# Block products (seven in place of eight) for the second FFN product in three of twelve chunks, and another order of splitting the attention probabilities

## Chip, core and metric

One core of a Trainium2 chip runs the whole program. The metric is the device time in microseconds (us), the median of three runs. Engines: PE is TensorE, DVE VectorE, ACT ScalarE, POOL GpSimd, SP the queue that issues DMAs.

## What is computed

The inputs are q, k, v of shape 4 x 8 x 768 x 64 (q and k are drawn eight times larger than usual) and the two FFN weights, 512 x 2048 and 2048 x 512. Everything is float32.

```
k_sum = k.reshape(B, H, 24, 32, D).max(axis=3);  v_sum = v.reshape(B, H, 24, 32, D).mean(axis=3)
scores = concat([where(|i - j| < 16, scale * q k^T, -1e9), scale * q k_sum^T + log(32)])
x = softmax(scores) @ concat([v, v_sum])          # heads side by side: 3072 tokens x 512
h = x @ w_in
out = (h * sigmoid(h)) @ w_out
```

## The kernel before

**Tiling.** The 3072 tokens are 12 chunks of 256 (CH). The hidden dimension is 16 tiles of 128 (NFT), called f here. For each chunk c and each f, `job_f` (L799) makes the first product (`ffn1`, L812): h, 128 hidden by 256 tokens, in one PSUM bank. Chunk 0 uses float32 matmuls. Every later chunk splits both operands in two float16 parts, high and low, and takes three of the four products, so a first product is 12 matmuls of 256 columns (L818). Then ACT writes t = tanh(h) (L842), DVE makes t = (t + 1) * h (L843), ACT rounds t to its high part gh (L845) and DVE subtracts to get the low part gl (L846). The second product (`ffn2`, L820) takes the two halves u of 128 tokens as stationary operand and the weight rows of f as the moving one: 3 matmuls of 512 columns for each u (L826). They are summed over the 16 f in two banks (4 and 5). At f = 15 the banks are scaled into a staging tile (L871, L872) and stored (L873).

**PSUM.** There are eight banks of 128 x 512 float32. From chunk 1 on h takes banks 0, 1 and 2 in turn (tag "late h"). Banks 6 and 3 hold scores and 7 the attention output. Bank keys of the plan are (bank, half).

**Attention** for chunk c + 2 runs beside chunk c, so none is left beside chunks 10 and 11. For a tile of 128 tokens the scores are made on PE (L591), masked with their row minimum on DVE (L627), and exponentiated with row sums on ACT (L630). In `job_a` (L609), late part, each of two heads' probabilities is scaled by its reciprocal sum into float16 (`scaled`, on DVE, ACT or POOL: L645, L641, L643) and its low part follows on DVE, head by head (`low`, L674). A DMA transposes both parts (L677). PE multiplies them with v (L709), and the result is split into xh and xl (L725, L726), the moving operand of the first product.

**Weights.** They are loaded and unpacked during chunk 0 (`job_load`, `job_w`), scaled by powers of two (`w_scale`, L775) and split into float16 high and low parts over their own storage (`job_pair`). The float32 copy of each weight tile, wr4[:, f, kind, :512], isn't read after that.

**Order of the work.** Nothing is issued in the order of the code. Each job gives `Plan.op` its possible engines with a cost in ns, what it reads and writes, and a due time made from i = 16 c + f and the offsets in TUNE (L960). `Plan.schedule` (L178) lays all operations out in time by these costs, forward and backward in six rounds; each takes the engine on which it would finish well. `Plan.issue` (L210) then emits them sorted by planned start. Each engine executes its own stream in that order, and waits on semaphores where data or storage needs it. A first product may run ahead of the second product by three f (APART, key "turn"). Costs on DVE and POOL exclude each other in the plan unless an operation says otherwise (port=()).

Of the kernel before, what the change touches and what calls it, by code (L numbers as in the profile page):

```python
# [22 lines left out]
P = 128  # L23
# [7 lines left out]
NKEY = HALF + BLK + NB  # L31
# [15 lines left out]
SHRINK = 2.0 ** -25  # L47
# [177 lines left out]
def local_attn_ffn(ctx: ExitStack, tc: tile.TileContext, qkT, qP, qF, kF, v, vR, vP, w, out):  # L225
    nc = tc.nc
    eng = {"dve": nc.vector, "act": nc.scalar, "pool": nc.gpsimd, "dma": nc.sync}
# [19 lines left out]
    wr4 = wr.rearrange("p (f k c) -> p f k c", f=NFT, k=2)  # L247
# [31 lines left out]
    first = const.tile([P, max(NP * 2 * UW + 8 * DM, 8 * KP)], F16, name="first")  # L279
    half = 8 * P + 8 * KT  # L280
# [328 lines left out]
    def job_a(m, prio):  # L609
# [11 lines left out]
        def sum_key(j, i):  # L621
            return ("sum", i4, j, i)
# [42 lines left out]
        for j, n in enumerate(ns):  # L665
            pk, et = (m + j) % NP, e_t[n]
            pt, (tt, ttk) = p_t[pk], tt_of(m + j)
            pkeys = [("p", pk, i) for i in range(2)]
            for i in range(2):
                plan.op({"dve": 235, "act": 296, "pool": 320}, lambda e, i=i, j=j, pt=pt: scaled(e, pt[:, i, :NKEY], j, i), r=[sum_key(j, i), ("e", n, i)], w=[pkeys[i]], prio=prio)  # L670

            def low(e, pt=pt, et=et, j=j):
                for i in range(2):
                    nc.vector.scalar_tensor_tensor(out=pt[:, i, P:P + NKEY], in0=et[:, i, :], scalar=su4[:, 2 * j + i:2 * j + i + 1], in1=pt[:, i, :NKEY], op0=ALU.mult, op1=ALU.subtract)  # L674

            plan.op({"dve": 510}, low, r=[sum_key(j, i) for i in range(2)] + [("e", n, i) for i in range(2)], w=pkeys, prio=prio)
# [98 lines left out]
    def w_scale(prio):  # L775
        plan.op({"dve": 80}, lambda e: nc.vector.tensor_reduce(out=wx_t, in_=wm_t, axis=AX.X, op=ALU.max), r=[("wm", f, kind) for f in range(NFT) for kind in range(2)], w=["wx"], prio=prio)
        k = sbank()

        def tr(e, k=k):
            for j in range(2):  # L780
                nc.tensor.transpose(out=bank[k][:1, j * P:(j + 1) * P], in_=wx_t[:, j:j + 1], identity=ident)

        plan.op({"pe": 220}, tr, r=["wx"], w=bk(k), prio=prio, cols=256)
        steps = (
            lambda e, k=k: nc.vector.tensor_reduce(out=wc[:, 0:2], in_=bank[k][:1, :2 * P].rearrange("o (a p) -> o a p", a=2), axis=AX.X, op=ALU.max),
            lambda e: nc.vector.tensor_scalar(out=wc[:, 0:2], in0=wc[:, 0:2], scalar1=1e-30, scalar2=None, op0=ALU.max),
            lambda e: nc.vector.tensor_scalar(out=wc[:, 2:4].bitcast(U32), in0=wc[:, 0:2].bitcast(U32), scalar1=0x7F800000, scalar2=None, op0=ALU.bitwise_and),
            lambda e: nc.vector.tensor_scalar(out=wc[:, 6:8], in0=wc[:, 2:4], scalar1=2.0 ** -14, scalar2=None, op0=ALU.mult),
            lambda e: nc.vector.reciprocal(out=wc[:, 4:6], in_=wc[:, 6:8]),
            lambda e: nc.vector.scalar_tensor_tensor(out=wc[:, 7:8], in0=wc[:, 6:7], scalar=1.0 / SHRINK, in1=wc[:, 7:8], op0=ALU.mult, op1=ALU.mult))  # L790
# [8 lines left out]
    def job_f(i, c, f):  # L799
# [138 lines left out]
    for i, (c, f) in enumerate(order):  # L938
        plan.slack = SLACK if i >= SETTLED else {}
        d = c + 2 if c + 2 < NCHUNK else None  # L940
        if d and c and f == 0:
            job_stage(2 * d)
            job_attn(2 * d, True)
            job_stage(2 * d + 1)
        plan.slack = {"pe": GATE_SLACK} if i >= SETTLED else {}
        job_f(i, c, f)
        plan.slack = SLACK if i >= SETTLED else {}
        if c == 0 and f == NFT - 1:
            spare[0] = 1
# [72 lines left out]
```

## Time and profile before

| | us |
|---|---|
| median of 3 runs (599.81 to 600.15) | 599.84 |
| the profiled execution, its own time | 599.46 |
| its span, first to last instruction | 597.8 |
| PE busy / DVE / ACT / POOL | 588.6 / 440.1 / 372.2 / 108.6 |
| PE idle in the span | 9.2 |

The profile shows one execution. Busy times are sums for an engine; a wait is put down to the event that came last. Rows of a timeline have start, duration, engine, line, operation, operands with shapes, and in brackets the idle time of the engine before it with what ended that. Matmuls overlap in the pipeline, so the next one starts before the printed duration is over. A group's idle time counts the engine's idle just before its instructions.

### The profile page before, as it was taken

The numbers are of one execution on the slowest core, as the hardware profiler recorded it, in microseconds if no ns is written. First come the engines' busy times: TensorE is split into PE (matmuls) and PEld (weight loads), VectorE is DVE, ScalarE is ACT, GpSimd is POOL, SyncE is SP. The second block draws the span as 40 slices with busy tenths as digits, with TensorE's granted clock in tenths as the row PEclk, the third lists the DMA queues.
The fourth block names the chain that finished last, engine by engine and source line by source line (L and its number), as shares of the span: only waits on it lengthen the run. The fifth ranks groups of instructions, "written<-read, shape, count | busy, mean of one in ns | idle before, by whom it ended". The sixth has DMA issues, their size and how long they took to land.

```text
span 597.8 us, 15304 instructions
## 1 busy us (share of the span) xinstructions
PE 588.6 (98%) x5848; PEld 399.7 (67%) x5848; DVE 440.1 (74%) x1338; ACT 372.2 (62%) x1014; POOL 108.6 (18%) x164
## 2 busy tenths in 40 slices
PE   8999999999999999999999999999999999999997
PEld 5666656676666666666666666666766766666664
DVE  6999979997886748979896555979898764333332
ACT  4998859777757756647675544756777554333332
POOL 3211201035421000043330020014241400000000
PEclk9999999999999999999999999999999999999999
DMA  8999532135765634543646530442734401000001
GB/s 334 410 420 412 174 123 98 27 87 152 153 128 172 157 90 128 90 133 97 123 129 174 166 89 36 120 122 62 169 93 106 111 2 36 36 1 2 35 1 37
DMA packets 60916, 75.29 MB, mean 126 GB/s; under 512 B 41914, under 2 KB 42170, under 8 KB 59050
## 3 DMA queue, kind: packets, MB, share of 16 engines
q1 hardware_dynamic: 60842, 74.31, 41.9%
q8 instruction: 46, 0.75, 0.5%
q14 instruction: 28, 0.23, 0.1%
HBM read 56.79 MB, written 6.29 MB: 106 GB/s over the span
## 4 chain that ended last, share of the span: by engine, by line
PE 82%; DVE 9%; DMA 4%; ACT 3%; issue 1%; SPq 1%; DVEq 0%; ACTq 0%
PE bank L826 37%; PE bank L818 37%; PE bank L709 3%; DVE wm L758 2%; PE bank L591 2%; DVE wr L757 2%; DMA raw<-in_qkT_dram 1%; DMA second<-in_qP_dram 1%; DVE e L627 1%; PE bank L694 1%; ACT wr L771 1%; PE bank L656 1%; DVE t L843 1%; PE bank L837 1%; DMA raw<-in_qF_dram 1%
## 5 line engine op out<-in xcount | busy, mean ns | idle before, releaser
L818 PE MATMUL bank<-x,wr 128*128 128x256 f16 x2112 | 258.1, 273 | 0.0
L818 PEld LDWEIGHTS <-wr 128*128 128x128 f16 x2112 | 205.6, 98 | 57.2 <-issue 0.6
L826 PE MATMUL bank<-wr,gh 128*128 128x512 f16 x702 | 209.1, 380 | 0.4 <-ACT gh L845 0.4
L843 DVE SCALAR_TENSOR_TENSOR t<-t,bank 128x256 f32<-128x256 f32 x192 | 80.1, 417 | 85.9 <-ACT t L842 85.0
L842 ACT ACTIVATE t<-bank,th 128x256 f32<-128x256 f32 x176 | 82.1, 467 | 92.7 <-PE bank L818 92.4
L826 PE MATMUL bank<-wr,gl 128*128 128x512 f16 x351 | 133.1, 379 | 0.1
L845 ACT ACTIVATE gh<-t 128x256 f16<-128x256 f32 x176 | 72.9, 414 | 72.3 <-DVE t L843 69.4
L846 DVE SCALAR_TENSOR_TENSOR gl<-t,gh 128x256 f16<-128x256 f32 x176 | 86.6, 493 | 40.4 <-ACT gh L845 40.0
L826 PEld LDWEIGHTS <-gh 128*128 128x128 f16 x702 | 65.9, 98 | 44.6 <-ACT gh L845 0.7
L630 ACT ACTIVATE e<-e,mx 128x120 f32<-128x120 f32 x192 | 73.2, 383 | 12.9 <-DVE mx L627 12.7
L826 PEld LDWEIGHTS <-gl 128*128 128x128 f16 x351 | 34.3, 98 | 43.7 <-DVE gl L846 3.0
L674 DVE SCALAR_TENSOR_TENSOR first<-e,sum,first 128x120 f16<-128x120 f32 x144 | 49.8, 394 | 0.3 <-POOL first L643 0.3
L643 POOL TENSOR_SCALAR first<-e,sum 128x120 f16<-128x120 f32 x52 | 22.0, 433 | 125.7 <-ACT gh L845 39.6
L627 DVE CUSTOM_DVE_ANT_0 e<-bank,masks,qsc 128x120 f32<-128x120 f32 x144 | 42.2, 336 | 2.8 <-PE bank L591 2.8
L630 ACT ACTIVATION_READ_ACCUMULATOR e<-e,mx 128x1 f32 x192 | 36.4, 190 | 0.0
L238 POOL TENSOR_TENSOR first<-raw,first 120x1024 f16<-120x1024 f32 x14 | 30.4, 2173 | 10.9 <-ACT first L231 5.4
L823 PE MATMUL bank<-wr,t 128*128 128x512 f32 x64 | 30.7, 599 | 0.0
L815 PE MATMUL bank<-x,wr 128*128 128x256 f32 x112 | 26.3, 379 | 0.0
L815 PEld LDWEIGHTS bank<-x,wr 128*128 128x128 f32 x112 | 21.0, 190 | 7.0 <-issue 4.1
L643 POOL TENSOR_SCALAR e<-e,sum 128x120 f32<-128x120 f32 x28 | 11.2, 412 | 71.4 <-DVE sum L636 61.8
L561 POOL TENSOR_SCALAR raw<-raw,vsc 120x1024 f32<-120x1024 f32 x10 | 11.7, 1167 | 55.5 <-PE bank L818 31.0
L773 DVE SCALAR_TENSOR_TENSOR wr<-wr,ws 128x1024 f16<-128x1024 f32 x16 | 20.2, 1274 | 0.1
(146 smaller groups left out, 598.1 us busy)
## 6 DMA issues: line engine op xcount, KB each, us to landing
wr<-in_w_dram SPq DMA_DIRECT2D x14, 1024.0 KB
raw<-in_qkT_dram SPq DMA_DIRECT2D x18, 576.0 KB
out_dram<-raw SPq DMA_DIRECT2D x23, 256.0 KB
raw<-in_kF_dram SPq DMA_DIRECT2D x12, 384.0 KB
raw<-in_qF_dram SPq DMA_DIRECT2D x9, 512.0 KB
raw<-in_vR_dram SPq DMA_DIRECT2D x12, 384.0 KB
raw<-in_v_dram SPq DMA_DIRECT2D x18, 208.0 KB
raw<-in_v_dram SPq DMA_DIRECT2D x18, 192.0 KB
```

The source lines that it names most:

```text
L627: plan.op({"dve": 262 if b else 206}, lambda e, i=i, j=j, et=et, mx=mx: nc.vector.tensor_tensor_reduce(out=et[:, i, :], in0=sc[j][:, i, :N ...
L630: plan.op({"act": 385}, lambda e, i=i, j=j, et=et, mx=mx: nc.scalar.activation(out=et[:, i, :], in_=et[:, i, :], func=AF.Exp, scale=-1.0, ...
L643: nc.gpsimd.tensor_scalar(out=out, in0=src, scalar1=by, scalar2=0.0, op0=ALU.mult, op1=ALU.add)
L674: nc.vector.scalar_tensor_tensor(out=pt[:, i, P:P + NKEY], in0=et[:, i, :], scalar=su4[:, 2 * j + i:2 * j + i + 1], in1=pt[:, i, :NKEY], o ...
L815: nc.tensor.matmul(out=h, lhsT=wi[:, ct * P:(ct + 1) * P], rhs=x0[:, ct, :], start=(ct == 0), stop=(ct == NCT - 1))
L818: nc.tensor.matmul(out=h, lhsT=wip[:, part, ct * P:(ct + 1) * P], rhs=x[:, ct, :], start=(ct == 0 and q == 0), stop=(ct == NCT - 1 and q = ...
L823: nc.tensor.matmul(out=bank[ob[u]], lhsT=t[:, u * P:u * P + P], rhs=wo, start=opens, stop=closes)
L826: nc.tensor.matmul(out=bank[ob[u]], lhsT=g[:, u * P:u * P + P], rhs=wop[:, part, :], start=(opens and q == 0), stop=(closes and q == 2))
L842: plan.op({"act": 264 if c == 0 else 360}, lambda e: nc.scalar.activation(out=t, in_=h, func=AF.Tanh, scale=0.5 if c == 0 else th[:, 0:1]) ...
L843: plan.op({"dve": 337}, lambda e: nc.vector.scalar_tensor_tensor(out=t, in0=t, scalar=1.0, in1=h, op0=ALU.add, op1=ALU.mult), r=bk(k), w=[ ...
L845: plan.op({"act": 311}, lambda e: nc.scalar.activation(out=gh, in_=t, func=AF.Copy, scale=SHRINK), r=[("t", j)], w=[("gh", n)], prio=post)
L846: plan.op({"dve": 343}, lambda e: nc.vector.scalar_tensor_tensor(out=gl, in0=t, scalar=SHRINK, in1=gh, op0=ALU.mult, op1=ALU.subtract), r= ...
```

## The change

**Second product in chunks 8, 9 and 10.** `job_fast` replaces `job_f` there and works on pairs of f. The second product of a pair is a 2 x 2 block product: token halves by the two f on the left, the two f by column halves (256 columns each) on the right. Eight block products are replaced by seven, with sums of blocks on both sides. On the left t of both f is kept in float32 (both f's h lie in the halves of bank 0), three blocks are split directly (hd, ld, 384 columns) and four sums of blocks are formed on POOL or DVE and split (hs, ls, 512 columns). On the right `job_quad` prepares four sums of weight blocks for each pair, between i = 88 and 116 by its place in the loop, and splits them into the storage of the float32 weights. The seven results, each 3 matmuls of 256 columns a pair, are summed over the eight pairs in 3.5 banks (1, 2, 4 and half of 5; in chunk 10: 3, 6, 7 and half of 5). At the end of a chunk one copy and four DVE additions combine them into the four output blocks; two stores follow. A pair's first products may start when the third pair before it is done ("turn").

**Probabilities.** Scaling is done in place in float32, then one operation copies both heads to the high part and one subtraction makes both low parts.

**Others.** The scale of the weights leaves two more bits of room, all values of TUNE differ, and "quad" is new.

```diff
+FAST = 8
+EARLY = 40
+PACE = 4
...
             for i in range(2):
-                plan.op({"dve": 235, "act": 296, "pool": 320}, ... scaled(e, pt[:, i, :NKEY], j, i), r=[sum_key(j, i), ("e", n, i)], w=[pkeys[i]], prio=prio)
-
-            def low(e, pt=pt, et=et, j=j):
-                for i in range(2):
-                    nc.vector.scalar_tensor_tensor(out=pt[:, i, P:P + NKEY], in0=et[:, i, :], scalar=..., in1=pt[:, i, :NKEY], op0=ALU.mult, op1=ALU.subtract)
-
-            plan.op({"dve": 510}, low, ..., w=pkeys, prio=prio)
+                plan.op({"dve": 160, "act": 296, "pool": 320}, ... scaled(e, e_t[n][:, i, :], j, i), r=[sum_key(j, i)], w=[("e", n, i)], prio=prio)
+            hi, lo = pt[:, :, :NKEY], pt[:, :, P:P + NKEY]
+            plan.op({"dve": 193, "act": 282, "pool": 360}, lambda e, hi=hi, et=et: copy(e, hi, et), r=ekeys, w=pkeys, prio=prio)
+            plan.op({"dve": 320, "pool": 600}, lambda e, hi=hi, lo=lo, et=et: less(e, lo, et, hi), r=ekeys, w=pkeys, prio=prio)
...
-scalar1=2.0 ** -14   (w_scale)
+scalar1=2.0 ** -12
...
+    def job_quad(g, i, prio):
+        fa, fb = 2 * g, 2 * g + 1
...
+        for n, x, y in ((0, b12, b11), (2, b22, b12), (1, b22, t[0]), (3, b21, t[1])):
+            plan.op({"pool": 740, "dve": 400}, lambda e, n=n, x=x, y=y: less(e, t[n], x, y), ...)
+        plan.op({"act": 990, "dve": 603}, ... hi = flat * by ...)
+        plan.op({"dve": 1196}, ... lo = flat * by - hi ...)
+
+    acc = {6: (0, 0), 2: (0, 1), 7: (1, 0), 5: (1, 1), 4: (2, 0), 3: (2, 1), 1: (3, 0)}
+    threes = [(1, 2, 4, 5)] * (NCHUNK - 2) + [(3, 6, 7, 5)]
...
+    def job_fast(i, c, f):
+        n, z, b = i % 2, c % 2, c * CH // S
+        g, j, th = f // 2, i // 2 % 3, th_t[b % 2]
+        h, hk = bank[0][:, n * CH:n * CH + CH], [("bank", 0, n)]
...
+        plan.op({"pe": 1312}, ffn1, r=[...] + [("turn", i - 5 - n)], w=hk, prio=i + nudge("f1", i), cols=3072, fill=fill)
+        plan.op({"act": 360}, ... tu = tanh(h) ..., r=hk + [...], w=tk, prio=post)
+        plan.op({"dve": 337}, ... tu = (tu + 1) * h ..., r=hk, w=tk, prio=post, port=())
+        if n == 0:
+            return
...
+        plan.op({"act": 430}, ... hd = src * SHRINK ..., r=tks, w=[("hd", j)], prio=post)
+        plan.op({"dve": 470}, ... ld = src * SHRINK - hd ...)
+        for m, x, y, op in ((0, a21, a22, ALU.add), (2, a11, a21, ALU.subtract), (1, sm[:, 0], a11, ALU.subtract), (3, a12, sm[:, 1], ALU.subtract)):
+            plan.op({"pool": 470, "dve": 210}, ..., r=tks, w=[("sm", j)], prio=post)
+        plan.op({"act": 540}, ... hs = sf * SHRINK ...)
+        plan.op({"dve": 610}, ... ls = sf * SHRINK - hs ...)
...
+                    for q, (x, p) in enumerate(((hi, 0), (hi, 1), (lo, 0))):
+                        nc.tensor.matmul(out=acc_of(c, m)[0], lhsT=x[:, left[m]], rhs=right[m](p), ...)
...
+        for ms, need in (((1,), direct), ((2, 6), ...), ((7, 5), ...), ((4, 3), ...)) if opens or closes else (((1, 4, 2), direct + mixed[2:]), ((6, 7, 5, 3), mixed + direct)):
+            ends = [("turn", i - 1), ("turn", i)] if ms[-1] == 3 else []
+            plan.op({"pe": 328 * len(ms)}, products(ms), ..., prio=late, cols=768 * len(ms))
+        if not closes:
+            return
...
+        plan.op({"act": 300, "dve": 332}, ... s1 = m1 * by ...)
+        plan.op({"dve": 660}, add(rows[:, 1:3], both(ka), spread(s1)), ...)
+        plan.op({"dve": 660}, add(u34, both(kb), spread(rows[:, 1])), ...)
+        plan.op({"dve": 393}, add(rows[:, 1], acc_of(c, 5)[0], u34[:, 0]), ...)
+        plan.op({"dve": 660}, add(rows[:, 0:4:3], both(kd), u34), ...)
...
-        job_f(i, c, f)
+        if i == NFT:
+            release("areas", [("wf", x, 0) for x in range(NFT)], FAST * NFT - TUNE["quad"])
+        g, rest = divmod(i - FAST * NFT + EARLY, PACE)
+        if 0 <= g < NFT // 2 and not rest:
+            job_quad(g, i, FAST * NFT + 2 * g - TUNE["quad"])
+        (job_fast if FAST <= c < NCHUNK - 1 else job_f)(i, c, f)
...
-TUNE = dict(vd=145.25, ws=-1296.0, ..., post=1219.25, ffn2=350.75, ..., qk=66.0, k=57.5, ...)
+TUNE = dict(quad=-364.0, vd=78.5, ws=-1986.25, ..., post=745.0, ffn2=542.75, ..., qk=644.25, k=431.25, ...)
```

## Rows read from the trace of the kernel before

**Rows 1.** The page: busy us of each engine with its share of the span and its instructions, and the granted TensorE clock in 40 equal slices, in tenths of full speed.
```profile
PE 588.6 (98%) x5848; PEld 399.7 (67%) x5848; DVE 440.1 (74%) x1338; ACT 372.2 (62%) x1014; POOL 108.6 (18%) x164
...
PEclk9999999999999999999999999999999999999999
```

**Rows 2.** What PE waited for over the whole span: us in total, times, longest.
```profile
PE bank L325 <- POOL ident masks.py:199: 1.4, 1, 1.4
PE bank L594 <- ACT raw L871: 1.0, 1, 1.0
...
PE bank L826 <- ACT gh L845: 0.4, 1, 0.4
```

**Rows 3.** Timeline of PE in chunk 11: start us, us, engine, line, operation, count.
```profile
560.08 1.47 PE L818 MATMUL bank<-x,wr 128*128 128x256 f16 x12
561.39 0.59 PE L826 MATMUL bank<-wr,gh 128*128 128x512 f16 x2
...
562.04 0.59 PE L826 MATMUL bank<-wr,gh 128*128 128x512 f16 x2
...
562.68 1.47 PE L818 MATMUL bank<-x,wr 128*128 128x256 f16 x12
```

**Rows 4.** Groups of instructions by line and shape, whole span: busy us, mean ns of one, idle before them.
```profile
L846 DVE SCALAR_TENSOR_TENSOR gl<-t,gh 128x256 f16<-128x256 f32 x176 | 86.6, 493 | 40.4 <-ACT gh L845 40.0
L843 DVE SCALAR_TENSOR_TENSOR t<-t,bank 128x256 f32<-128x256 f32 x192 | 80.1, 417 | 85.9 <-ACT t L842 85.0
L674 DVE SCALAR_TENSOR_TENSOR first<-e,sum,first 128x120 f16<-128x120 f32 x144 | 49.8, 394 | 0.3 <-POOL first L643 0.3
L773 DVE SCALAR_TENSOR_TENSOR wr<-wr,ws 128x1024 f16<-128x1024 f32 x16 | 20.2, 1274 | 0.1
L238 DVE TENSOR_TENSOR first<-raw,first 120x1024 f16<-120x1024 f32 x4 | 4.9, 1220 | 0.1
...
L238 POOL TENSOR_TENSOR first<-raw,first 120x1024 f16<-120x1024 f32 x14 | 30.4, 2173 | 10.9 <-ACT first L231 5.4 <-DVE first L235 4.6
```

**Rows 5.** Busy us of each engine in the stretches of chunks 8, 9 and 10, by the first products' starts; then granted clock, DMA share, GB/s.
```profile
416.20:462.80 46.60, 46.14 (x527) 30.98 (x526) 42.46 (x170) 33.30 (x114) 12.19 (x16) 1.00 0.53 126
462.80:507.00 44.20, 44.20 (x476) 30.45 (x475) 27.93 (x80) 22.50 (x62) 7.00 (x7) 1.00 0.21 52
507.00:549.70 42.70, 42.70 (x338) 28.98 (x337) 15.37 (x35) 15.21 (x34) 0.00 (x0) 1.00 0.04 13
```

**Rows 6.** Timeline of the end. L856 is the last second product, made in two column halves of one bank: three matmuls from 593.28 into the first, three from 593.61 into the second. L871 reads the first half, L872 the second.
```profile
593.50 0.27 PE L856 MATMUL bank<-wr,gl 128*128 128x256 f16 x1
...
593.83 0.27 PE L856 MATMUL bank<-wr,gl 128*128 128x256 f16 x1
594.14 0.47 ACT L871 ACTIVATE raw<-bank,th 128x256 f32<-128x256 f32 x1 [0.56 <-PE bank L856]
594.64 0.48 DVE L872 TENSOR_SCALAR raw<-bank,th 128x256 f32<-128x256 f32 x1 [3.74 <-ACT raw L871]
```

**Rows 7.** Timeline near the start. L627 reads scores of the second half of a bank, L656 transposes into the first half of it.
```profile
13.20 0.28 DVE L627 CUSTOM_DVE_ANT_0 e<-bank,masks 128x120 f32<-128x120 f32 x1
...
13.43 0.62 PE L656 MATMUL bank<-ident,e 128*120 128x128 f32 x4 [0.21 <-DVE mx L627]
```

**Rows 8.** Timeline in chunk 11: one first product, its tanh and its L843.
```profile
567.89 1.47 PE L818 MATMUL bank<-x,wr 128*128 128x256 f16 x12
...
569.47 0.47 ACT L842 ACTIVATE t<-bank,th 128x256 f32<-128x256 f32 x1 [1.23 <-PE bank L818]
...
569.97 0.42 DVE L843 SCALAR_TENSOR_TENSOR t<-t,bank 128x256 f32<-128x256 f32 x1 [1.28 <-ACT t L842]
```

**Rows 9.** PE's attention matmuls in chunk 8 (416.2 to 462.8): groups by line, busy us, mean ns.
```profile
L591 PE MATMUL bank<-second 64*64 64x120 f16 x144 | 2.5, 215 | 0.0
L709 PE MATMUL bank<-third,first 120*64 120x64 f16 x96 | 1.9, 197 | 0.0
```

**Rows 10.** Timeline: the first and the last of the 16 first products of chunk 7, each with its L843.
```profile
366.21 1.47 PE L818 MATMUL bank<-x,wr 128*128 128x256 f16 x12
...
368.29 0.42 DVE L843 SCALAR_TENSOR_TENSOR t<-t,bank 128x256 f32<-128x256 f32 x1 [2.09 <-ACT t L842]
...
407.87 1.47 PE L818 MATMUL bank<-x,wr 128*128 128x256 f16 x12
...
410.43 0.42 DVE L843 SCALAR_TENSOR_TENSOR t<-t,bank 128x256 f32<-128x256 f32 x1 [0.23 <-ACT t L842]
```

**Rows 11.** Timeline: the first, the third and the last of the 8 first products in the first half of chunk 9, each with its L843.
```profile
462.80 1.47 PE L818 MATMUL bank<-x,wr 128*128 128x256 f16 x12
...
464.81 0.42 DVE L843 SCALAR_TENSOR_TENSOR t<-t,bank 128x256 f32<-128x256 f32 x1 [0.79 <-ACT t L842]
...
467.69 1.47 PE L818 MATMUL bank<-x,wr 128*128 128x256 f16 x12
...
472.29 0.41 DVE L843 SCALAR_TENSOR_TENSOR t<-t,bank 128x256 f32<-128x256 f32 x1
...
482.69 1.47 PE L818 MATMUL bank<-x,wr 128*128 128x256 f16 x12
...
484.76 0.42 DVE L843 SCALAR_TENSOR_TENSOR t<-t,bank 128x256 f32<-128x256 f32 x1 [1.88 <-ACT t L842]
```

More of the change, by code (lines that the diff above doesn't have):

```diff
@@ L669, in job_a @@
             for i in range(2):
-                plan.op({"dve": 235, "act": 296, "pool": 320}, lambda e, i=i, j=j, pt=pt: scaled(e, pt[:, i, :NKEY], j, i), r=[sum_key(j, i), ("e", n, i)], w=[pkeys[i]], prio=prio)
-            def low(e, pt=pt, et=et, j=j):
-                for i in range(2):
-                    nc.vector.scalar_tensor_tensor(out=pt[:, i, P:P + NKEY], in0=et[:, i, :], scalar=su4[:, 2 * j + i:2 * j + i + 1], in1=pt[:, i, :NKEY], op0=ALU.mult, op1=ALU.subtract)
-            plan.op({"dve": 510}, low, r=[sum_key(j, i) for i in range(2)] + [("e", n, i) for i in range(2)], w=pkeys, prio=prio)
+                plan.op({"dve": 160, "act": 296, "pool": 320}, lambda e, i=i, j=j, n=n: scaled(e, e_t[n][:, i, :], j, i), r=[sum_key(j, i)], w=[("e", n, i)], prio=prio)
+            ekeys = [("e", n, i) for i in range(2)]
+            hi, lo = pt[:, :, :NKEY], pt[:, :, P:P + NKEY]
+            plan.op({"dve": 193, "act": 282, "pool": 360}, lambda e, hi=hi, et=et: copy(e, hi, et), r=ekeys, w=pkeys, prio=prio)
+            plan.op({"dve": 320, "pool": 600}, lambda e, hi=hi, lo=lo, et=et: less(e, lo, et, hi), r=ekeys, w=pkeys, prio=prio)
             plan.op({"dma": 1250}, lambda e, tt=tt, pt=pt: nc.sync.dma_start_transpose(out=tt, in_=pt.rearrange("p a b -> p (a b)")), r=pkeys + ["third"], w=[ttk], prio=prio)
@@ L787, in w_scale @@
             lambda e: nc.vector.tensor_scalar(out=wc[:, 2:4].bitcast(U32), in0=wc[:, 0:2].bitcast(U32), scalar1=0x7F800000, scalar2=None, op0=ALU.bitwise_and),
-            lambda e: nc.vector.tensor_scalar(out=wc[:, 6:8], in0=wc[:, 2:4], scalar1=2.0 ** -14, scalar2=None, op0=ALU.mult),
+            lambda e: nc.vector.tensor_scalar(out=wc[:, 6:8], in0=wc[:, 2:4], scalar1=2.0 ** -12, scalar2=None, op0=ALU.mult),
             lambda e: nc.vector.reciprocal(out=wc[:, 4:6], in_=wc[:, 6:8]),
@@ L873, in job_f, with area, sums_of @@
                 plan.op({"dma": 820 * size}, lambda e, o=o, r0=r0, cs=cs: nc.sync.dma_start(out=out[r0:r0 + P, cs], in_=o), r=okey, prio=i - TUNE["out"])
+    def area(f, kind, dt):
+        return wr4[:, f, kind, :DM].bitcast(dt)
+    def sums_of(g):
+        return [area(2 * g + part, 1, F16).rearrange("p (n c) -> p n c", n=4) for part in range(2)]
+    def job_quad(g, i, prio):
+        prio += nudge("quad", g)
+        fa, fb = 2 * g, 2 * g + 1
+        a, key = 12 + 2 * (g % 2), [("quad", g % 2)]
+        flat = wr4[:, a:a + 2, 0, :DM].bitcast(F32)
+        t = [flat[:, n // 2, n % 2 * CH:n % 2 * CH + CH] for n in range(4)]
+        b11, b12, b21, b22 = (area(f, 1, F32)[:, cs] for f in (fa, fb) for cs in (slice(0, CH), slice(CH, DM)))
+        for n, x, y in ((0, b12, b11), (2, b22, b12), (1, b22, t[0]), (3, b21, t[1])):
+            plan.op({"pool": 740, "dve": 400}, lambda e, n=n, x=x, y=y: less(e, t[n], x, y), r=[("wf", fa, 1), ("wf", fb, 1), "areas", ("turn", i - 4)], w=key, prio=prio)
+        hi, lo = (area(f, 1, F16).rearrange("p (n c) -> p n c", n=2) for f in (fa, fb))
+        by = ws_t[:, 1:2]
+        plan.op({"act": 990, "dve": 603}, lambda e: nc.scalar.activation(out=hi, in_=flat, func=AF.Copy, scale=by) if e == "act" else
+                nc.vector.tensor_scalar(out=hi, in0=flat, scalar1=by, scalar2=None, op0=ALU.mult), r=key + ["ws"], w=[("wf", fa, 1), ("sh", g)], prio=prio)
+        plan.op({"dve": 1196}, lambda e: nc.vector.scalar_tensor_tensor(out=lo, in0=flat, scalar=by, in1=hi, op0=ALU.mult, op1=ALU.subtract), r=key + ["ws", ("sh", g)], w=[("wf", fb, 1), ("sl", g)], prio=prio)
@@ L957, in local_attn_ffn @@
     plan.issue()
-TUNE = dict(vd=145.25, ws=-1296.0, s0=-1306.0, wp=-955.25, wm=1695.25, km=296.75, w_dma=-551.75, w_dec=-1473.75, a0=-15.0, a1=-399.75, d1=7.75, span=34.25, post=1219.25, ffn2=350.75, jc0=150.5, jc1=208.75, jx0=-166.75, jx1=-108.0, vs=25.0, qk=66.0, k=57.5, v=2313.0, v0=-101.0, out=-36.75, first=771.75)
+TUNE = dict(quad=-364.0, vd=78.5, ws=-1986.25, s0=-1447.25, wp=-974.5, wm=1315.75, km=19.25, w_dma=-222.0, w_dec=-1042.25, a0=-36.5, a1=-651.75, d1=136.75, span=9.75, post=745.0, ffn2=542.75, jc0=660.25, jc1=94.5, jx0=-302.0, jx1=-38.5, vs=-0.25, qk=644.25, k=431.25, v=2292.5, v0=6.5, out=173.25, first=823.25)
 NUDGE = {}
```

65 lines of the change are left out of this document (added).

## The prediction

> **What bounds the kernel now.** I read the page's busy times first. PE is busy 588.6 of 597.8 us at the full granted clock, 2.4 GHz throughout [rows 1]. A busy PE proves little by itself, so the next view was what PE waited for. After the first 100 us it waited once, 0.4 us for a gh of ACT; the other entries lie in the start [rows 2]. The 9.2 us that PE is not busy are 3.7 us behind the last matmul (it ends at 594.10 of 597.8) [rows 6] and some 5.5 us in the first 92 us. So PE's own instructions bound the time, and removed PE time comes off the end, as long as nothing new makes PE wait.
>
> The timeline of the last chunk gives the price of those instructions [rows 3]. A first product (12 matmuls of 256 columns) runs from 560.08 to 561.39, 1.31 us or 109.2 ns a matmul. A half of a second product (3 matmuls of 512 columns) takes 0.65 us (561.39 to 562.04), and a whole f takes 562.68 - 560.08 = 2.60 us. So the two halves take 2.60 - 1.31 = 1.29 us.
>
> **What the change does to PE.** For two f the second product is 4 x 0.647 = 2.59 us now. Afterwards it is 7 products x 3 matmuls of 256 columns in f16, the shape of the first product: 21 x 109.2 = 2.29 us. That is 0.30 us less for a pair, and 24 pairs (8 in each of chunks 8 to 10) give **-7.2 us**. The first product, the attention matmuls, and chunks 1 to 7 and 11 keep their instructions.
>
> **What it adds elsewhere.** On DVE a pair costs 2 x (0.417 + 0.493) = 1.82 us now [rows 4]. Afterwards the two L843 remain (0.83), and two low-part subtractions of 384 and 512 columns replace the two L846. No row has these widths: between 493 ns at 256 columns and 1274 at 1024 [rows 4] the slope is 1.02 ns a column, so an estimate of 0.62 and 0.75. That is +0.39 a pair. The four 128-column sums have no row either: a 1024-column subtraction takes 1220 ns on DVE and 2173 on POOL [rows 4]. An eighth of that plus a fixed part is some 0.25 or 0.45 each (an estimate), so 0 to 1.0 us of DVE a pair, depending on which engine the plan picks. The prepared weight sums are 8 x 1.27 on DVE plus 8 wide conversions and 32 quarter subtractions on ACT and POOL, from chunk 5 on. The block results at a chunk's end need three more DVE passes over PSUM, each under 0.75. ACT has one conversion of 384 and one of 512 columns for two of 256. The probabilities lose two L674 (0.39 each) and gain one copy and one subtraction over 240 columns: -0.2 to +0.1 a head pair. I cost all of it at nothing, because these engines have room: in chunk 9 DVE is busy 27.9 of 44.2 us and in chunk 10 15.4 of 42.7 [rows 5]. Chunk 8 has none (42.5 of 46.6), so there attention will slide later; it is due only by chunk 10 or 11. If that cover failed, the price would be the 0.4 to 1.4 us a pair, 3 to 11 us for chunk 8.
>
> The start is re-ordered too, as nearly all due times change. Only its idle 5.5 us can be gained there, and as much may be lost; no row favours either sign, so I take 0 and keep +-2 for the range. No DMA is added but two output stores a chunk, as before; they leave late and are waited for by nobody in the loop.
>
> **The new wait.** Now three whole banks take turns for the first product's result (late h). In the changed chunks both f of a pair use the two halves of bank 0. The planner treats the halves as separate. The trace does not: at the end ACT's read of one half of a bank starts at 594.14, after the matmuls into the other half (593.83 + 0.27), not after its own (593.50 + 0.27); and DVE's read of the other half waits for ACT's to end, 594.64 [rows 6]. At the start PE's transpose (13.43) waits for a DVE read at a place where only the other half of its bank is being read [rows 7]. So engines are held apart by bank, also for two reads. The Trainium skill (PSUM — Partial Sum Buffer, PSUM bank collisions raise a hardware error) says that two engines must not touch one bank and quadrant at once, reads and disjoint columns included, and are to be ordered by semaphores; the trace agrees, with DVE held from 594.14 to 594.61 by ACT's read of the other half. By the planner's view of separate halves the sum below would be -7.2, by that rule it holds the term for the wait.
>
> What follows. I call the stretch from a first product's end to the end of its L843 a pass. Undisturbed it is 1.02 us: matmuls end 569.36, ACT 569.47, DVE ends 570.39 [rows 8]. As issue follows planned start, the second f's matmuls are issued ahead of the first f's tanh. So tanh waits for both, then tanh, L843, tanh, L843 run one behind the other: two passes, some 2.1 us, before the next pair may write bank 0. Between two pairs of first products PE has one pair's block products, 2.29 us. Undisturbed it fits, by 0.2 us: the 12 pairs from 483 us on have no attention beside them, and I cost the wait there at 0 (at most 0.3 a pair, if the new wide DVE operations get in between). The 12 pairs before them, chunk 8 and the first half of 9, have attention on ACT and DVE. PE's attention matmuls there add cover, 2.5 + 1.9 = 4.4 us in 46.6 [rows 9], 0.5 a pair, so some 2.8 in all. The length of a pass under load has two rows to go by. In chunk 7 it goes from 1.0 to 1.5, 16 of them, mean 1.31 [rows 10]: two passes make 2.6, no wait. In the first half of chunk 9 eight passes have mean 2.02, the third 3.5 [rows 11]: 4.0, a wait of 1.2. Ends: 0 and 12 x 1.2 = 14 us. I take **0.25 us a pair, +3.0 us**, near chunk 7: today's long passes are those of a queue that may run late because three banks cover it, while a plan with less lead puts tanh and L843 ahead of attention, and each wait of PE lets the queues drain.
>
> **Sum.** -7.2 + 3.0 = -4.2 us. Against the profiled execution's 599.46 us that is 595.3; the median of the runs shown, 599.84, stands 0.38 above it, so **595.6 us**.
>
> **Rivals.** (a) *The products in full*: bank 0 never holds PE, as in the undisturbed passes [rows 8], or the start gains what bank 0 takes. -7.2 gives 592.6. For it speaks that half of the pairs are undisturbed, against it the passes of rows 11. (b) *A wash*: 0.5 to 0.6 us a loaded pair, or 0.25 and a start worse by 3: 598.6 to 601, say 599.8. (c) *Slower, through bank 0*: the passes stay as long as in the first half of chunk 9, the four operations behind each other behind attention, PE in order behind them. It decides from 7.2 / 12 = 0.6 us a loaded pair, that is from passes of 1.7 us on. At the rows' 2.0 the price is 12 x 1.2 = 14.4, a loss of 7.2: 607; half of that excess gives 603. Chunk 8's DVE, busy 91%, speaks for it; that attention isn't due speaks against. That the change doesn't do what it says (matmuls of 256 columns slower with two different stationary operands) I give no chance of its own: the first product has that shape and changes its stationary operand at every matmul.
>
> **How the numbers follow.** Forecast, 593.5 to 598.6: 0.45. (a) 0.2. (b) 0.13. (c) 0.22. Under 0.2% (1.2 us) a measurement of this kernel cannot tell from no change, so faster is 0.45 + 0.2 = 0.65, same 0.13, slower 0.22. The range reaches below to (a) with a better start, 591.5, and above through (b) into the milder half of (c), 602.5.
>
> **What would show it.** PE's block products would take 2.29 us a pair, back to back, and each changed chunk some 2.4 us less of PE's busy time. If the wait is as I say, the list of what PE waited for gets a row of the changed first product behind DVE's L843 counterpart, some 3 us in all, nearly all of it before the middle of chunk 9, and tanh of a pair's first f starts only after the second f's matmuls. The forecast is wrong if that row exceeds 7 us (c), if it is missing (a), if PE waits instead for the mixed sums of DVE or POOL, or if the first 92 us change by more than 2 us.

## Result: slower by 0.8%, and the profile after

| | before | after |
|---|---|---|
| median of 9 runs, us | 599.81 | 604.27 (602.55 to 608.63) |
| ratio, 95% interval | | 1.0076 [1.0051, 1.0100] |
| profiled execution, its span | 599.46, 597.8 | 606.30, 604.6 |
| PE busy / idle in the span | 588.6 / 9.2 | 585.0 / 19.6 |

The forecast was 595.6 us with a range to 602.5, and 65% on faster. It came out slower, on the side of rival (c). The profiled execution lies 2.0 us above the median; a load at the start is waited for 1.7 us longer in it than before.

In the kernel after, the changed chunks have lines of their own: L915 is a first product, L910 a filler matmul just ahead of one, L920 its tanh and L921 its multiplication (L842 and L843 before), L928 and L929 the split of the three direct blocks, L932 the sums, L934 and L935 their split, L946 the block products. The page, as [rows 1]:

```profile
PE 585.0 (97%) x6076; PEld 423.7 (70%) x6076; DVE 453.2 (75%) x1256; ACT 399.6 (66%) x1070; POOL 227.4 (38%) x343
```

PE does less work and still ends later, so the next view is what it waited for. As [rows 2]: us in total, times, longest.

```profile
PE bank L915 <- DVE wr L921: 3.0, 5, 1.9
PE bank L597 <- DMA second<-in_qP_dram: 2.6, 1, 2.6
PE bank L910 <- DVE wr L921: 2.4, 1, 2.4
PE bank L695 <- ACT third L234: 1.9, 1, 1.9
...
PE bank L915 <- ACT wr L920: 0.8, 1, 0.8
```

The first, third and last of these rows are the wait at bank 0, 6.2 us, where the forecast had 3.0 and named 7 as the point at which it would be wrong. The other two rows lie in the first 92 us. The windows say where bank 0 costs: the stretches of chunks 8, 9 and 10, with the columns of [rows 5].

```profile
423.20:468.90 45.70, 40.06 (x520) 34.64 (x519) 31.28 (x93) 31.25 (x87) 29.21 (x46) 1.00 0.37 97
468.90:513.70 44.80, 44.39 (x602) 38.77 (x601) 32.89 (x96) 29.32 (x88) 32.82 (x47) 1.00 0.25 62
513.70:556.80 43.10, 42.89 (x431) 38.02 (x429) 27.55 (x58) 18.76 (x38) 11.61 (x22) 1.00 0.10 26
```

PE idles 5.64 us in chunk 8, 0.41 in chunk 9 and 0.21 in chunk 10. From the start of chunk 8 to that of chunk 11 the kernel after takes 133.6 us, the one before 133.5 [rows 5]: the products' gain is used up here, and what remains of the loss lies ahead of it: in this execution chunk 1 starts 4.6 us later (92.4 against 87.8), and chunks 1 to 7 take 2.4 us more (330.8 against 328.4).

The timeline of chunk 8's first five pairs shows how (start, duration, engine, line, operation, and in brackets the idle time before with what ended it):

```profile
423.23 2.78 PE L915 MATMUL bank<-x,wr 128*128 128x256 f16 x24
425.94 0.82 PE L594 MATMUL bank<-second 64*64 64x120 f16 x48
426.05 0.47 ACT L920 ACTIVATE wr<-bank,th 128x256 f32<-128x256 f32 x1 [2.48 <-PE bank L915]
426.56 0.42 DVE L921 SCALAR_TENSOR_TENSOR wr<-wr,bank 128x256 f32<-128x256 f32 x1 [2.38 <-ACT wr L920]
427.01 0.47 ACT L920 ACTIVATE wr<-bank,th 128x256 f32<-128x256 f32 x1 [0.49 <-DVE wr L921]
427.54 1.47 PE L915 MATMUL bank<-x,wr 128*128 128x256 f16 x12 [0.77 <-ACT wr L920]
429.12 0.42 DVE L921 SCALAR_TENSOR_TENSOR wr<-wr,bank 128x256 f32<-128x256 f32 x1 [0.88 <-PE bank L915]
429.59 1.47 PE L915 MATMUL bank<-x,wr 128*128 128x256 f16 x12 [0.58 <-DVE wr L921]
431.10 0.47 ACT L920 ACTIVATE wr<-bank,th 128x256 f32<-128x256 f32 x1 [0.72 <-PE bank L915]
431.60 0.42 DVE L921 SCALAR_TENSOR_TENSOR wr<-wr,bank 128x256 f32<-128x256 f32 x1 [0.17 <-ACT wr L920]
432.51 0.45 ACT L920 ACTIVATE wr<-bank,th 128x256 f32<-128x256 f32 x1
433.00 0.42 DVE L921 SCALAR_TENSOR_TENSOR wr<-wr,bank 128x256 f32<-128x256 f32 x1 [0.25 <-ACT wr L920]
433.47 1.03 PE L910 MATMUL bank<-ident 128*128 128x256 bf16 x8 [2.41 <-DVE wr L921]
434.34 2.78 PE L915 MATMUL bank<-x,wr 128*128 128x256 f16 x24
436.96 0.49 PE L946 MATMUL bank<-wr 128*128 128x256 f16 x3
...
440.24 2.78 PE L915 MATMUL bank<-x,wr 128*128 128x256 f16 x24
442.86 2.46 PE L946 MATMUL bank<-wr 128*128 128x256 f16 x21
...
444.61 2.12 POOL L241 TENSOR_TENSOR first<-raw,first 120x1024 f16<-120x1024 f32 x1 [1.85 <-DVE wr L929]
444.71 2.10 DVE L648 TENSOR_SCALAR e<-e,sum 128x120 f32<-128x120 f32 x1
...
446.73 0.41 DVE L921 SCALAR_TENSOR_TENSOR wr<-wr,bank 128x256 f32<-128x256 f32 x1
447.19 2.78 PE L915 MATMUL bank<-x,wr 128*128 128x256 f16 x24 [1.87 <-DVE wr L921]
```

Three things are to be read here. First, three engines take turns at one bank, one at a time: at 427.54 PE writes the first half while the multiplication of the second half stands and waits, it comes at 429.12, and PE's second half only behind it. Second, ahead of the third pair PE has nothing else to do: the first block product of the chunk starts at 436.96. A pair may start when the third pair before it is done, so at the chunk's start three pairs follow each other with 0.8 us of attention between them. Two passes take 2.4 us (431.06 to 433.42), PE idles for 2.41 and then runs 8 filler matmuls, 0.87 us. Third, at 444.71 one of the new in-place scalings stands on DVE for 2.10 us, for all of POOL's subtraction beside it (its median is 0.28), and the second multiplication of the pair behind it. That is the wait of 1.87. With the 0.77, 0.58 and 2.41 ahead of it, these waits are the 5.6 us of chunk 8.

### The profile page after: what moved, and what is told of

Its sections match the earlier page's. It is cut to its first block, busy times and chain, and to the rows that moved or that the text cites. A ratio compares the mean times of both kernels' runs of the same rounds, so it can differ in the third digit from the quotient of the medians.

```text
span 604.6 us, 15827 instructions
## 1 busy us (share of the span) xinstructions
PE 585.0 (97%) x6076; PEld 423.7 (70%) x6076; DVE 453.2 (75%) x1256; ACT 399.6 (66%) x1070; POOL 227.4 (38%) x343
## 4 chain that ended last, share of the span: by engine, by line
PE 76%; DVE 8%; ACT 8%; DMA 4%; POOL 2%; issue 2%; SPq 1%; DVEq 0%; ACTq 0%
PE bank L827 25%; PE bank L819 25%; PE bank L915 10%; PE bank L946 7%; PE bank L710 2%; PE bank L594 2%; ACT wr L772 2%; DVE wr L758 1%; DVE wm L759 1%; DMA second<-in_qP_dram 1%; DVE e L630 1%; ACT wr L752 1%; ACT wr L756 1%; ACT e L633 1%; DMA wr<-in_w_dram 1%
## 5 line engine op out<-in xcount | busy, mean ns | idle before, releaser
L819 PEld LDWEIGHTS <-wr 128*128 128x128 f16 x1536 | 149.5, 98 | 41.4 <-issue 1.1
L827 PE MATMUL bank<-wr,gh 128*128 128x512 f16 x510 | 151.9, 380 | 0.0
L843 ACT ACTIVATE t<-bank,th 128x256 f32<-128x256 f32 x128 | 59.9, 468 | 61.0 <-PE bank L819 60.5
L827 PE MATMUL bank<-wr,gl 128*128 128x512 f16 x255 | 96.6, 379 | 0.0
L847 DVE SCALAR_TENSOR_TENSOR gl<-t,gh 128x256 f16<-128x256 f32 x128 | 66.1, 519 | 20.9 <-ACT gh L846 19.9
L846 ACT ACTIVATE gh<-t 128x256 f16<-128x256 f32 x128 | 52.7, 413 | 42.6 <-DVE t L844 40.4
L646 POOL TENSOR_SCALAR e<-e,sum 128x120 f32<-128x120 f32 x74 | 33.7, 465 | 116.3 <-DVE sum L639 44.8
L915 PE MATMUL bank<-x,wr 128*128 128x256 f16 x576 | 67.0, 272 | 3.8 <-DVE wr L921 3.0
L915 PEld LDWEIGHTS <-wr 128*128 128x128 f16 x576 | 56.0, 98 | 11.9 <-issue 5.0
L946 PE MATMUL bank<-wr 128*128 128x256 f16 x504 | 59.1, 273 | 0.0
L932 POOL TENSOR_TENSOR wr<-wr 128x128 f32<-128x128 f32 x69 | 39.9, 589 | 44.3 <-DVE wr L932 29.4
L946 PEld LDWEIGHTS <-wr 128*128 128x128 f16 x504 | 49.0, 98 | 6.0 <-issue 0.2
L241 POOL TENSOR_TENSOR first<-e,first 128x240 f16<-128x240 f32 x63 | 44.0, 709 | 11.9 <-ACT first L234 10.3
L920 ACT ACTIVATE wr<-bank,th 128x256 f32<-128x256 f32 x48 | 22.5, 471 | 33.9 <-PE bank L915 28.7
L921 DVE SCALAR_TENSOR_TENSOR wr<-wr,bank 128x256 f32<-128x256 f32 x48 | 19.9, 419 | 33.3 <-ACT wr L920 32.3
```

Source lines behind the costliest of these rows:

```text
L241: eng[e].tensor_tensor(out=out, in0=in0, in1=in1, op=ALU.subtract)
L819: nc.tensor.matmul(out=h, lhsT=wip[:, part, ct * P:(ct + 1) * P], rhs=x[:, ct, :], start=(ct == 0 and q == 0), stop=(ct == NCT - 1 and q = ...
L827: nc.tensor.matmul(out=bank[ob[u]], lhsT=g[:, u * P:u * P + P], rhs=wop[:, part, :], start=(opens and q == 0), stop=(closes and q == 2))
L843: plan.op({"act": 264 if c == 0 else 360}, lambda e: nc.scalar.activation(out=t, in_=h, func=AF.Tanh, scale=0.5 if c == 0 else th[:, 0:1]) ...
L846: plan.op({"act": 311}, lambda e: nc.scalar.activation(out=gh, in_=t, func=AF.Copy, scale=SHRINK), r=[("t", j)], w=[("gh", n)], prio=post)
L847: plan.op({"dve": 343}, lambda e: nc.vector.scalar_tensor_tensor(out=gl, in0=t, scalar=SHRINK, in1=gh, op0=ALU.mult, op1=ALU.subtract), r= ...
```

## Experiments

Theory A: the shared bank turned the gain into a loss. Theory B: the bank costs little, and the added work or the new order does it. Theory C: the new start and due times carry a share of their own. All ratios are to the kernel before on the same chip.

**Own banks.** The changed kernel with its plan untouched; the two f of a pair write h into two different banks. To free one, block product 1 is added into the place of product 2, by as many matmuls as before, so this kernel leaves the separate sum of product 1 out.

```diff
-        h, hk = bank[0][:, n * CH:n * CH + CH], [("bank", 0, n)]
+        h, hk = bank[n][:, :CH], [("bank", 0, n)]
...
+        at, side = (k, half) if m != 1 else (threes[c][0], 1)
+        return bank[5 if at == 1 else at][:, side * CH:side * CH + CH], ("bank", k, half)
```

> The changed kernel with the same plan and the same instructions, but the first products of a pair go to two banks (0 and 1) instead of the halves of bank 0. To free a bank, block product 1 is summed into the place of product 2, so the sums are not the reference's; PE's work is the same. Theory A (the shared bank makes PE wait): the waits of PE for tanh and the following multiplication, 6.2 us in the changed kernel, fall under 1.5 us, and the median lies 4 to 6 us under the changed kernel's 604.3. Rival B (ACT and DVE are late in chunk 8 whatever the banks, since POOL and DVE block each other): these waits stay above 4 us and the median falls by less than 2 us.

Measured: 595.74 us (594.55 to 600.01), 0.9928 [0.9905, 0.9951]. Its stretches of chunks 8, 9 and 10:

```profile
419.90:459.80 39.90, 39.44 (x520) 34.57 (x519) 32.47 (x95) 32.12 (x90) 29.94 (x48) 1.00 0.48 113
459.80:503.60 43.80, 43.80 (x602) 38.69 (x600) 35.20 (x95) 29.12 (x88) 32.32 (x46) 1.00 0.29 65
503.60:546.20 42.60, 42.60 (x431) 38.06 (x430) 27.20 (x57) 17.87 (x35) 10.76 (x20) 1.00 0.09 24
```

Together 126.3 us, against 133.5 before: -7.2, the products' term. That the tenth agrees is luck: the first products run ahead of the block products, so the ends of the stretches shift, and from the start of chunk 1 to the end it is 503.4 against 510.0 us, -6.6. Of the waits from chunk 8 to 10 one of 0.5 us is left. The medians put the bank at 604.27 - 595.74 = 8.5 us; the stretches at 133.6 - 126.3 = 7.3. Theory A holds and B falls: all the added work of DVE, ACT and POOL is in this kernel, the scaling that stands behind POOL too (its longest is 2145 ns), and with a bank for each f PE waits for none of it beyond that 0.5 us.

**The bank alone.** The kernel before, with h of chunks 8 to 10 in two banks, once as two whole ones and once as the halves of bank 0. The plan is the same for both.

```diff
         if 8 <= c <= 10:
-            h, hk = bank[i % 2][:, :CH], bk(i % 2)
+            h, hk = bank[0][:, i % 2 * CH:i % 2 * CH + CH], [("bank", i % 2, half) for half in range(2)]
```

> The kernel before, with first products of chunks 8 to 10 in two whole banks in turn instead of three. Theory A: two whole banks cover a pass of up to 3.9 us, so at most 1 us slower than before, in chunk 8. Rival B: passes of 3.3 us on average with peaks of 6 make PE wait already here, 3 us or more.

> The same plan as the run with two banks, instruction by instruction, but the first products of chunks 8 to 10 alternate between the halves of one bank. Theory A: PE waits 0.5 to 1.5 us at most of the 16 first products of chunk 8 and some of chunk 9, in all 8 to 20 us over the run with two banks, and under 1 us in chunk 10, where a pass of 1.02 us fits into the 1.29 us of the second product. If halves of a bank were independent, the two runs would agree within 0.5 us.

Measured: two banks 601.30 us, 1.0019 [1.0001, 1.0036]; one bank 609.38 us (607.33 to 610.59), 1.0143 [1.0110, 1.0176]. One bank less costs 1.5 us, a little more than theory A's 1; the sharing costs 8.1 us more, with not one block product in the kernel. By the stretches of chunks 8 to 10 it is 141.0 against 134.3 us, 6.7. Its waits of PE from chunk 8 on (here L821 is the first product, L813 its filler, L845 tanh, L846 the multiplication; L829 is the second product):

```profile
PE bank L821 <- ACT t L845: 2.7, 3, 1.2
PE bank L813 <- ACT t L845: 1.7, 1, 1.7
PE bank L821 <- DVE t L846: 1.5, 2, 0.9
```

That is 5.9 us in six waits, so not at most of chunk 8's 16 first products, as forecast, but in sum much as in the changed kernel.

**No block products.** The changed kernel with `job_f` in all chunks: only the splitting and the due times are left.

```diff
-        (job_fast if FAST <= c < NCHUNK - 1 else job_f)(i, c, f)
+        job_f(i, c, f)
```

> The changed kernel without block products and without the prepared weight sums: chunks 8 to 10 run the old way, the new due times and the new splitting of the probabilities stay. Theory C (the re-ordered start costs): chunk 1 begins 3 to 5 us later than before, and the time is 3 to 6 us above before (603 to 606). Rival D (the late start of the profiled execution was that one execution's): within 1.2 us of before, and the whole loss belongs to chunks 8 to 10.

Measured: 602.53 us, 1.0043 [1.0024, 1.0061]. In its profiled execution (605.27 us) chunk 1 starts at 92.8 us (before: 87.8), and 0.8 more is lost later; but this execution is 2.7 us above its median, and the median is below theory C's 603. Theory C holds in part.

**Which part of it.** Three kernels swap one of the rest: the changed one with the old due times (all of TUNE), the one before with the new due times, the one before with the new splitting of the probabilities.

> The changed kernel with the due times (TUNE) of before, and quad as in the change. Theory C (the new due times cost 2.8 us at the start): chunk 1 begins at 88 to 89 us instead of 90.6 to 92.4, and the time falls by 2 to 3 us, if chunks 8 to 10 wait as much as now (601 to 602). Rival E (the new splitting of the probabilities changes the plan of the start, whatever the due times): chunk 1 begins at 90 us or later and the time stays within 1.5 us of 604.

> The kernel before with the due times of after, nothing else. Theory C: chunk 1 begins 2 to 4 us later than before's 87.8, the time is 2 to 4 us above before. Rival E: within 1 us of before.

> The kernel before with the new splitting of the probabilities and its own due times. Theory C: within 1 us of before, as neither POOL nor DVE bounds the time there. Rival E: 2 to 4 us above before, by a later start of chunk 1 or by POOL's subtractions (0.64 us each) holding up DVE.

Measured: 610.13 us, 1.0171 [1.0141, 1.0201]; 610.26, 1.0172 [1.0139, 1.0205]; 605.00, 1.0091 [1.0058, 1.0123]. None of the three lies where theory C or rival E had it; each is slower. The first two say above all that a set of due times fits one program: the old set costs the changed kernel 5.9 us, the new one the kernel before 10.6, most of it after the start. The third loses 5.3 us, of which 0.8 by its later chunk 1 in the profiled execution; why the rest is lost was not followed up. For the start the profiled executions give chunk 1 at 89.4, 89.4 and 88.6 us. Plans like the one before start it at 87.2 to 88.7 (three executions), the kernels with both new parts at 89.6 to 92.8 (seven), so each part seems to take about half of some 3 us. Single executions spread by 1.5 to 3 us here, and I leave the split open.

**Telling the plan.** If the plan's two separate halves are the fault, one key for the bank should mend it.

```diff
-        h, hk = bank[0][:, n * CH:n * CH + CH], [("bank", 0, n)]
+        h, hk = bank[0][:, n * CH:n * CH + CH], bk(0)
```

> The changed kernel, complete, but the plan is told that a first product and its readers hold both halves of bank 0. The order changes, the instructions don't. Theory A: with the bank as one resource the plan puts block products between the two first products of a pair, so a pass of 1.0 us stands against 1.0 to 1.3 us of other PE work; PE's waits for tanh and the multiplication fall from 6.2 us to 1 to 4 us and the time lies 2 to 6 us under the changed kernel's 604.3 (598 to 602). Rival B (not the order, but too few banks for any order): no gain, 603 to 607.

Measured: 643.15 us, 1.0714 [1.0689, 1.0738], far outside both forecasts. Now the plan itself keeps one f's first product back until the other's multiplication is done: 287 filler matmuls instead of 65, and each changed chunk takes 58 to 60 us. In its waits one row has 13 entries:

```profile
PE bank L910 <- DVE wr L921: 11.5, 13, 1.5
```

**Both f at once.** The other cure is to hold the bank for less time: one tanh and one multiplication over all 512 columns. First with the plan untouched (the first f's two operations emit nothing, the second's do both), then planned as such. In the first the kept order issues some pairs' first product ahead of the wide operations, so these take the next pair's h.

```diff
-        plan.op({"act": 360}, ... tu = tanh(h) ..., r=hk + [...], w=tk, prio=post)
-        plan.op({"dve": 337}, ... tu = (tu + 1) * h ..., r=hk, w=tk, prio=post, port=())
         if n == 0:
             return
+        tks = [("tp", j, 0), ("tp", j, 1)]
+        plan.op({"act": 600}, ... t = tanh(bank[0]) ..., r=bk(0) + [...], w=tks, prio=post)
+        plan.op({"dve": 605}, ... t = (t + 1) * bank[0] ..., r=bk(0), w=tks, prio=post, port=())
```

> The changed kernel once more, on the same chip as the two runs that follow. Median 603 to 605; if its profiled execution has a PE wait under 1 us for the first q instead of 2.6, chunk 1 begins at 90.6 us, as in the run with own banks, which has the same plan; chunks 8 to 10 take 133 to 134 us between the starts of chunks 8 and 11 and PE waits some 6 us for tanh and the multiplication there.

> The changed kernel with its plan and order, complete; tanh and the multiplication of a pair's first f emit nothing, and those of the second f do both halves of bank 0 in one instruction of 512 columns each. Theory A: the four operations behind each other (2.1 us) become two (0.1 + 0.7 + 0.7 = 1.5 us), against 2.29 us of block products; PE's waits there fall from 6.2 us to 1 to 4, and the time lies 2 to 6 us under the changed kernel on the same chip (598 to 602). Rival B (ACT and DVE are late in chunk 8 whatever the bank): less than 1.5 us.

> As the run before, but the plan has the two wide operations as such, so the order of everything is laid out anew under the due times of the change. Theory A: PE's waits in chunks 8 to 10 are 0 to 3 us. A new layout under due times made for another program has cost 5 to 10 us in two runs above, so the time may lie anywhere from 597 to 610; what counts is the waits in chunks 8 to 10.

Measured on one chip: the changed kernel again 606.64 us (604.00 to 607.85), 1.0113 [1.0091, 1.0136]; both at once with its plan 598.22, 0.9975 [0.9964, 0.9986]; both planned 599.29 (598.21 to 602.24), 1.0000 [0.9986, 1.0014]. The changed kernel is slower here than its forecast of 603 to 605: in its profiled execution PE waits 7.5 us at the bank and chunks 8 to 10 take 136.6 us. The planned version takes back 7.3 us of it (5.0 of the 604.27 measured first) and ends level with the kernel before; its order is laid out anew, so not all of that need be the bank's. Both at once keeps the order: there PE waits 2.7 us at the bank, and chunks 8 to 10 take 128.9 us, where the kernel after takes 133.6 and own banks 126.3. The planned version's two wide operations (busy us, mean ns, idle before):

```profile
L923 ACT ACTIVATE wr<-bank,th 128x512 f32<-128x512 f32 x24 | 16.5, 686 | 21.0 <-PE bank L915 20.9
L924 DVE SCALAR_TENSOR_TENSOR wr<-wr,bank 128x512 f32<-128x512 f32 x24 | 16.4, 683 | 16.7 <-ACT wr L923 16.6
```

0.69 + 0.68 us a pair stand where 2 x (0.47 + 0.42) = 1.78 stood, and there are two turns at the bank in place of four. PE still waits 2.2 us at the bank, and 27 filler matmuls stand ahead of its first products in place of 8:

```profile
PE bank L910 <- DVE wr L924: 1.6, 2, 1.3
...
PE bank L915 <- DVE wr L924: 0.6, 1, 0.6
```

Of the kernels that compute the whole, none beats the one before by more than a measurement can tell.

## Why the prediction was wrong

**The products: right.** -7.2 us by 24 pairs; with own banks the three chunks are 7.2 us shorter, and all from chunk 1 to the end 6.6. The sign of 2.4 us less PE work in each changed chunk doesn't show by stretches: PE's busy time falls by 6.7, 0.4 and 0.1 us there (46.14 to 39.44, 44.20 to 43.80, 42.70 to 42.60), as the first block product of chunk 8 comes late and later ones slide into the next stretch. With the bank shared too, a pair's block products take what they should: 466.55 to 468.89 in the profiled execution, 2.34 us until the next first product.

**The added work at nothing: right as a cost, wrong as a neighbour.** By itself it costs nothing in chunks 8 to 10, as own banks shows, and attention slid out of chunk 8 as forecast (DVE busy 42.46 us there before, 31.28 after). The splits came out at 0.68 and 0.75 us for the estimated 0.62 and 0.75, the sums at 0.59 on POOL and 0.33 on DVE for 0.45 and 0.25 (busy us, mean ns, idle before):

```profile
L929 DVE SCALAR_TENSOR_TENSOR wr<-wr 128x384 f16<-128x384 f32 x24 | 16.3, 679 | 0.4
L935 DVE SCALAR_TENSOR_TENSOR wr<-wr 128x512 f16<-128x512 f32 x24 | 18.0, 750 | 7.0 <-ACT wr L934 7.0
L932 POOL TENSOR_TENSOR wr<-wr 128x128 f32<-128x128 f32 x69 | 39.9, 589 | 44.3 <-DVE wr L932 29.4 <-DVE wr L921 11.2 <-DVE sum L639 2.1
L932 DVE TENSOR_TENSOR wr<-wr 128x128 f32<-128x128 f32 x27 | 8.2, 333 | 0.3
```

But where the bank is shared, what stands ahead of a multiplication on DVE is paid by PE: the 1.87 us at 447.19.

**The start at 0 +- 2: wrong by about 3 us.** Own banks is 4.1 us faster than the kernel before and not 7.2; no blocks is 2.7 us slower. Their chunk 1 starts 2.8 and 5.0 us later, that of the kernel after 4.6, so the sign of a first 92 us changed by more than 2 us came. The traces show three parts of it, which no run takes singly. First, at one place PE waits for ACT's copy of `third`: 1.9 us in the kernel after, 2.2 in own banks and 2.3 in the changed kernel again, which have one plan; before, 0.7. Second, in the profiled execution of the kernel after, PE waits 2.6 us for a load, before 1.0; own banks and the changed kernel again wait 0.7 there, so this part belongs to the execution. Before:

```profile
PE bank L594 <- DMA second<-in_qP_dram: 1.0, 1, 1.0
PE bank L694 <- ACT third L231: 0.7, 1, 0.7
```

Third, behind such a wait the granted clock is lower, part of the time at 1.2 GHz (the third column from the end). In the kernel after that is behind the load, which lands at 8.63, in own banks behind the wait of 2.2 us, which ends at 68.88; before, the clock is 1.00 in both places.

```profile
8.00:11.00 3.00, 2.37 (x66) 2.29 (x67) 1.30 (x6) 0.87 (x4) 0.00 (x0) 0.66 1.02 415
11.00:14.00 3.00, 3.00 (x39) 2.26 (x40) 1.25 (x6) 0.77 (x3) 0.37 (x1) 0.78 1.04 415
```

```profile
70.00:75.00 5.00, 5.00 (x13) 2.73 (x13) 3.75 (x5) 2.12 (x5) 0.00 (x0) 0.66 0.73 261
```

At full clock these stretches would hold up to 1.7 us more of PE's work each, an estimate from the three rows (3 x 0.34 + 3 x 0.22, and 5 x 0.34). The prediction looked for a gain or loss in PE's idle time alone.

**The wait at bank 0: the step that failed.** The mechanism was as written: engines held apart by bank, tanh of both f behind both first products, four operations in a row. The rule of the Trainium skill (PSUM — Partial Sum Buffer, PSUM bank collisions raise a hardware error), that engines are to be ordered by bank, not by address, agrees with the 0.88 us for which the multiplication at 429.12 waits for a write into the other half. The term was mis-sized: +3.0 us, and 6.3 us of idle PE in the profiled execution, 6.7 to 8.5 by the experiments. It was also in another place. I spread 0.25 us over 12 loaded pairs because "between two pairs of first products PE has one pair's block products, 2.29 us". That holds for the undisturbed 12 pairs and for chunk 9, where the waits are as small as forecast. It does not hold at the start of chunk 8, which has no block products yet: the first five pairs take 5.6 us of the 6.3. The "turn" of three pairs, which the diff gave, said so, and the prediction makes no use of it: it lets three pairs of first products through one bank with next to nothing between them. The length of the passes was forecast well: over the 12 loaded pairs two passes take 2.5 us in the mean of the profiled execution (1.7 to 4.1), and the forecast had 2.6 and 4.0 as its ends; the cover was missing. Behind the second cause, DVE held by POOL, two passes take 4.12 us (443.02 to 447.14), near the upper end [rows 11].

Three readings behind the term were loose. In chunk 7 passes go from 1.0 to 2.1 us, not to 1.5 (the mean of 1.31 is right). Chunk 8's own passes in the kernel before, 3.29 us in the mean and 5.97 at the longest, were left out; two of them would have given 6.6 us, so the argument that long passes are those of a queue that may run late was borne out. And in [rows 7] the transpose starts 0.05 us before the printed end of the read that it is said to wait for; that engines are held apart by bank rests on [rows 6], and now on the run with one bank.

**The account.** -7.2 (products) + 8.5 (bank 0) + 3.1 (start: 7.2 - 4.1) = +4.4, and +4.46 measured. The last two both come from own banks, so this sum closes by itself; with the terms of other kernels it is -7.2 + 8.1 (one bank against two) + 2.7 (no blocks) = +3.6. By their intervals the differences for the bank are uncertain by some 2 us each. By the bank alone the change would have been near a wash; it seems that the start gave it its sign. Rival (c) named the mechanism, but by evenly long passes in 12 pairs; 7 us over 12 pairs are 0.58 us a pair, at its break-even of 0.6.

## What to carry to other kernels

Two results that share a bank cost what their readers take one after the other, unless other work stands between the writes; look for the place where that cover runs out (the first pairs of a phase), not at the mean. Either give each result a bank or read both with one wide operation: the first was worth 8.5 us here, the second 5.0 to 7.3 together with a new order. A gain of 7.2 us by fewer matmuls is also of the size of what else changes with it, some 3 us for a re-ordered start and 5.9 and 10.6 for due times made for another program, so try each part by itself.

## What was not expected of the hardware

**A scaling on DVE that stands behind POOL.** Before, the same scaling with a float16 result took at most 452 ns on DVE. In place in float32 it takes 282 at the median and 1146 to 2143 at four places, beside POOL's subtraction of 2.1 us at three of them, the case above among these, and beside a POOL scaling of 1.05 us at the fourth. The Trainium skill (SBUF — State Buffer, Who interferes with whom) has VectorE and GpSimd share a port pair that one operation holds until it ends, a tensor_scalar among those that may claim it; the trace agrees, 2.10 us beside 2.12. The hold itself is not new: in the kernel before the low-part subtractions stood behind POOL in the same way, up to 2.30 us for L674, and PE waited for none of it. The lines give the shortest, median and longest in ns, the first of the kernel before, the second of the kernel after:

```profile
L674 DVE SCALAR_TENSOR_TENSOR first<-e,sum,first x144: 305/336/2300, 151.7 to 495.5; 128x120 f16<-128x120 f32 x144
L648 DVE TENSOR_SCALAR e<-e,sum x46: 260/282/2143, 172.7 to 511.5; 128x120 f32<-128x120 f32 x46
```

None of the 47 scalings on DVE of the kernel before ran beside a subtraction of 2.1 us, so it is not shown that the type of the result makes the difference.

**PE's clock after a wait.** In the second profiled execution of the changed kernel the same wait of 2.4 us ends at 432.07, and from 431 to 437 the granted clock lies at 0.71 and 0.72 (the third column from the end), so part of that time ran at the lower level, 1.2 GHz:

```profile
428.00:431.00 3.00, 1.47 (x12) 1.17 (x12) 2.80 (x16) 2.11 (x7) 0.78 (x3) 1.00 0.57 182
431.00:434.00 3.00, 1.93 (x10) 1.37 (x10) 2.75 (x11) 3.00 (x12) 2.23 (x4) 0.71 0.91 209
434.00:437.00 3.00, 3.00 (x21) 2.35 (x20) 0.49 (x1) 0.97 (x2) 1.73 (x4) 0.72 0.27 65
```

There its 8 fillers take 1.71 us, and 1.03 in the first execution, whose clock stays at 1.00 through the same place:

```profile
432.00:435.00 3.00, 1.53 (x15) 1.36 (x14) 2.75 (x13) 3.00 (x13) 1.92 (x4) 1.00 0.59 129
```

So a wait of this length may be paid twice. The runs go with the clock: of the six of the changed kernel again, the one with a mean granted clock of 1.000 took 604.00 us and the one with 0.991 took 607.76. Of the 12 runs of the kernel before on the chip of the three swaps, the two at 0.997 took 602.28 and 602.53 us, the ten at 0.999 and 1.000 598.82 to 600.46. The nine runs of the kernel after have 0.993 to 0.999, so a part of its loss is likely the clock's; how large a part was not measured.
